# Transposing k, q and the attention result by DMA instead of on TensorE, in a fused attention and feed-forward kernel

## The chip, the cores and the metric

The kernel runs on one core of one Trainium2 chip. The metric is the device time of one execution, in microseconds (us). Every time is the median of some runs of the same program; every run here lists the core's mean granted TensorE clock and a state, and verdicts use fast runs alone. A ratio is the mean time of one kernel's fast runs over the mean of the other's fast runs in the same rounds, so it is not quite the ratio of the medians quoted.

Engine names in the profile: PE is TensorE's matmuls, PEld its weight loads, DVE is VectorE, ACT is ScalarE, POOL is GpSimd, and SP (SPq for its instruction queue) is SyncE.

## The reference

Sliding-window attention with a distance bias (8 batches, 8 heads, 576 positions, head size 64), then a feed-forward layer with a squared ReLU on the 4608 tokens.

```python
scores = scale * np.matmul(q, k.transpose(0, 1, 3, 2))
bias = slopes[:, None, None] * (-np.abs(rel).astype(np.float32))[None, :, :]
mask = (rel >= 0) & (rel < window)                  # window = 128
scores = np.where(mask, scores + bias[None], -1000000000.0)
attn = softmax(scores); attn_out = np.matmul(attn, v)
x = np.ascontiguousarray(attn_out.transpose(0, 2, 1, 3)).reshape(B * S, H * D)
h = x @ w_in                                        # 512 -> 2048
r = np.maximum(h, 0.0)
return ((r * r) @ w_out).astype(np.float32)         # 2048 -> 512
```
(softmax is written out in the original.) The kernel computes in bf16 with fp32 accumulation.

## The kernel before

Each batch has five blocks of positions (four of 128 and one of 64), 40 blocks in all. k and q of a block are loaded with positions on the partitions. Both must have the head dimension on the partitions, so TensorE transposes them against an identity into PSUM (eight 128x128 transposes, tile `tp`), and VectorE and ScalarE copy them out. q goes into `qp`, a tile with zeros in it, so that one matmul serves two heads. The attention result `x` of a block is transposed the same way (four transposes, tile `xp`) into `xT`, which the feed-forward layer reads.

```python
slot = Slot("h" if first else "att")
for i in range(2 * C):                               # C = 4
    def emit(i=i):
        ...
        nc.tensor.transpose(slot.tile[:, i * 128:(i + 1) * 128],
                            src[:, (i % C) * 128:(i % C + 1) * 128], ident)
    last = plan.add({"PE": mm(128)}, due - 56, emit, ...)
def evac_k():
    copy(t_k, kT[sk.idx][:, :, 0:n], slot.tile[:, 0:512]...)
t_k = plan.add(both if first else {"DVE": both["DVE"]}, due - 56, evac_k, [last], [], [slot])
for c2 in range(2):                                  # one half of qp on DVE, one on ACT
    def evac_q(c2=c2): ...
# ... scores, exp, mask, P x V, normalise into xt ...
for c in range(C):
    nc.tensor.transpose(slot_x.tile[:, c * 128:(c + 1) * 128], xt[sx.idx][:, c * 128:(c + 1) * 128], ident)
copy(t_xT[b, kb], xT[:, :, t0:t0 + n], slot_x.tile[:, 0:512]...)
```

Nothing is issued in the order of this text. Every operation is a task with an assumed duration, a key (its urgency) and the buffers that it takes and frees. A list scheduler in the kernel (class `Plan`) runs through assumed time and fixes, before the kernel starts, the order of instructions on every engine. An engine then works in that order and waits wherever the chip is later than the plan assumed.

The softmax here doesn't subtract the row's maximum and nothing guards it: scores larger than these inputs give would overflow.

Of the kernel before, what the change touches and what calls it, by code (L numbers as in the profile page):

```python
# [9 lines left out]
BF16 = mybir.dt.bfloat16  # L10
# [19 lines left out]
class Slot:  # L30


    def __init__(self, tag):
        self.tag, self.tile, self.left, self.freed, self.idx = tag, None, 0, 0.0, 0


class Plan:
# [18 lines left out]
    def order(self):  # L56
        used = {tag: [] for tag in self.bufs}
        free = {}
        cand = {}
        left = {}  # L60
        for t in self.tasks:
            left[t] = len(t.deps)
            for d in t.deps:
                d.users.append(t)
            for e in t.engs:
                free.setdefault(e, self.BEGIN.get(e, 800.0))
                cand.setdefault(e, [])
        for t in self.tasks:
            if not left[t]:
                for e in t.engs:  # L70
                    cand[e].append(t)

        def avail(t):
            at = t.ready
            for s in t.acq:
                u = used[s.tag]
                n = self.bufs[s.tag]
                if len(u) >= n:
                    old = u[len(u) - n]
                    if old.left:  # L80
                        return None
                    at = max(at, old.freed)
            return at

        done = []
        n_all = len(self.tasks)
        while len(done) < n_all:
            best = None
            for e, c in cand.items():
                lo = None  # L90
                for t in c:
                    a = avail(t)
                    if a is None:
                        continue
                    st = max(a, free[e])
                    k = (st, t.key, t.seq)
                    if lo is None or k < lo[0]:
                        lo = (k, t)
                if lo is not None and (best is None or lo[0][0] < best[0]):
                    best = (lo[0][0], e, lo[1])  # L100
            if best is None:
                raise RuntimeError("plan is stuck: " + repr([
                    (e, t.key, [s.tag for s in t.acq if avail(t) is None]) for e, c in cand.items() for t in c
                    if e != "POOL"][:40]))
            st, e, t = best
            t.eng, t.start = e, st
            dur = t.engs[e]
            if t.dma is not None:
                at = max(st + dur + 900.0, self.dma_free)
                self.dma_free = at + t.dma  # L110
                t.end = self.dma_free + 900.0
            else:
                t.end = st + dur + (self.LAT[e] if t.lat is None else t.lat)
            free[e] = st + dur
            for x in t.engs:
                cand[x].remove(t)
            for s in t.acq:
                s.idx = len(used[s.tag]) % self.bufs[s.tag]
                used[s.tag].append(s)
            for s in t.rel:  # L120
                s.left -= 1
                s.freed = max(s.freed, t.end)
            for u in t.users:
                left[u] -= 1
                u.ready = max(u.ready, st + dur if e == "PE" and "PE" in u.engs else t.end)
                if not left[u]:
                    for x in u.engs:
                        cand[x].append(u)
            done.append(t)
        done.sort(key=lambda t: (t.start, t.seq))  # L130
        return done
# [3 lines left out]
def kernel(  # L135
    ctx: ExitStack, tc: tile.TileContext, q, k, v, moe_w_in, moe_w_out, out
):
    nc = tc.nc

    B, H, S, D = q.shape  # L140
# [8 lines left out]
    C = d_model // 128  # L149
# [5 lines left out]
    psum = ctx.enter_context(tc.tile_pool(name="psum", bufs=2, space=bass.MemoryType.PSUM))  # L155
    work = ctx.enter_context(tc.tile_pool(name="work", bufs=2))

    ident = const.tile([128, 128], BF16)
# [5 lines left out]
    xT = const.tile([128, C, NT], BF16)  # L164

    def ring(name, n, shape):
        return [const.tile(shape, BF16, name=f"{name}_{i}") for i in range(n)]



    size = {"kn": 4, "qn": 4, "v": 6, "kT": 4, "qp": 3, "P": 3, "x": 2}
    kn = ring("kn", size["kn"], [128, d_model])
    qn = ring("qn", size["qn"], [128, d_model])
    vt = ring("vt", size["v"], [128, H, D + 1])
    kT = ring("kT", size["kT"], [128, C, 128])
    qp = ring("qp", size["qp"], [128, C, 2, 128])
    Pt = ring("P", size["P"], [128, H, 2, 128])
    xt = ring("x", size["x"], [128, d_model])

    plan = Plan({"h": 2, "o": 2, "s": 2, "att": 2, "rec": 4, "rt": 3, "g": 2, "osb": 3, **size})  # L180

    def act(n):
        return n * 0.84 + 55.0

    def dve(n, rate=1):
        return n / rate / 0.96 + 72.0

    def mm(n):
        return max(n, 64) / 2.4 + 1.5
# [12 lines left out]
    t_ident = plan.add({"DVE": 230.0}, -9e5 - 1, build_ident, [t_iota])  # L202
# [21 lines left out]
    t_zero = plan.add({"DVE": 2000.0}, -9e5, zero)  # L224
# [32 lines left out]
    s_in, t_in = {}, {}  # L257
# [23 lines left out]
    t_xT = {}  # L281
    chain = {"tp": [], "s": [], "pv": [], "xp": []}

    def copy(task, o, i):
        if task.eng == "DVE":
            nc.vector.tensor_copy(o, i)  # L286
        else:
            nc.scalar.activation(o, i, AF.Copy)  # L288

    def attention(m):  # L290
        b, kb = divmod(m, NKB)
        n = blk[kb]
        due = (b * S + kb * 128 + n) / 4 - 192 - 150
        first = b == 0


        sk, sq = Slot("kT"), Slot("qp")
        sk_of[m] = sk
        slot = Slot("h" if first else "att")
        last = None  # L300
        for i in range(2 * C):
            def emit(i=i):
                nm = "kq"[i // C]
                src = (kn if i < C else qn)[s_in[m, nm].idx]
                if i == 0:
                    slot.tile = psum.tile([128, 1024], BF16, tag=slot.tag, name="tp")
                nc.tensor.transpose(slot.tile[:, i * 128:(i + 1) * 128], src[:, (i % C) * 128:(i % C + 1) * 128],  # L307
                                    ident)
            last = plan.add({"PE": mm(128)}, due - 56, emit,
                            [last, t_ident, t_in[m, "kq"[i // C]]] + ([t_in[m, "q"]] + chain["tp"] if i == 0 else []),  # L310
                            [slot, sk, sq] if i == 0 else [], [s_in[m, "kq"[i // C]]] if i % C == C - 1 else [])
        chain["tp"] = [last]

        def evac_k():
            copy(t_k, kT[sk.idx][:, :, 0:n], slot.tile[:, 0:512].rearrange("p (c s) -> p c s", c=C)[:, :, 0:n])
        both = {"ACT": act(C * n), "DVE": dve(C * n, 2)}
        t_k = plan.add(both if first else {"DVE": both["DVE"]}, due - 56, evac_k, [last], [], [slot])
        t_q = []
        for c2 in range(2):
            def evac_q(c2=c2):  # L320
                po = c2 * 64
                o = qp[sq.idx][po:po + 64, :, c2, 0:n]
                i_ = slot.tile[po:po + 64, 512:1024].rearrange("p (c s) -> p c s", c=C)[:, :, 0:n]
                copy(t_q[c2], o, i_)
            t_q.append(plan.add(both if first else {"ACT": both["ACT"]} if c2 else {"DVE": both["DVE"]},
                                due - 56, evac_q, [last, t_zero], [], [slot]))
        t_k_of[m] = t_k


# [41 lines left out]
        sx = Slot("x")  # L371
        t_norm = []
        for hf in range(2):
# [32 lines left out]
            def norm(slot_v=slot_v, srec=srec, hf=hf):  # L406
# [5 lines left out]
                    op=ALU.mult)  # L412
            t_norm.append(plan.add({"DVE": dve(256)}, due - 12 + 4 * hf, norm, [t1] + t_norm,
                                   [], [slot_v, srec]))
        slot_x = Slot("o" if first else "att")
        last = None
        for c in range(C):
            def emit(c=c):
                if c == 0:
                    slot_x.tile = psum.tile([128, 1024], BF16, tag=slot_x.tag, name="xp")  # L420
                nc.tensor.transpose(slot_x.tile[:, c * 128:(c + 1) * 128],  # L421
                                    xt[sx.idx][:, c * 128:(c + 1) * 128], ident)
            last = plan.add({"PE": mm(128)}, due, emit, [last] + t_norm,
                            [slot_x] if c == 0 else [], [sx] if c == C - 1 else [])

        def evac():
            t0 = b * S + kb * 128
            copy(t_xT[b, kb], xT[:, :, t0:t0 + n],
                 slot_x.tile[:, 0:512].rearrange("p (c t) -> p c t", c=C)[:, :, 0:n])
        t_xT[b, kb] = plan.add(both if first else {"DVE": both["DVE"]}, due, evac, [last], [], [slot_x])  # L430

    sk_of, t_k_of = {}, {}
    for m in range(NBLK):
# [118 lines left out]
```

## Time and profile before

350.79 us, median of the 3 runs taken first (350.79 to 350.97).

| | before |
|---|---|
| PE busy, share of the span | 94% |
| DVE / ACT / POOL busy | 57% / 58% / 31% |
| share of PE in the chain of waits | 87% |
| tp and xp transposes in that chain | 4.8% and 2.3% |

The page of the kernel before: busy time by engine, the DMA queues (packets, megabytes, and the time their packets took as a share of 16 engines' span), and the chain of work that ended last.

```profile
...
PE 329.7 (94%) x2451; PEld 186.9 (54%) x2496; DVE 198.2 (57%) x600; ACT 203.2 (58%) x392; POOL 107.3 (31%) x133
...
q0 software_dynamic: 116736, 18.36, 72.0%
q1 hardware_dynamic: 5184, 9.44, 7.3%
...
PE 87%; DVE 6%; ACT 5%; issue 1%; ACTq 0%
PE o L483 34%; PE h L454 33%; PE ps_s L341 8%; PE tp L307 5%; PE pv L382 4%; PE xp L421 2%; ACT qp_90 L288 1%; DVE P_92 L367 1%; ACT masks L216 1%; ACT qp_91 L288 1%; ACT rt L462 1%; DVE x_96 L408 0%; ACT P_93 L359 0%; DVE qp_91 L286 0%; AC
...
```

TensorE bounds the kernel: it is busy 94% of the time and makes up 87% of the chain. The chain also prices the transposes: `tp` 5%, `xp` 2%.

The table by stage of the kernel before: for each stretch of time, its length, the busy time of each engine with the number of instructions, the granted clock, the DMA share (packet times summed over the 16 engines, so that overlapping packets can bring it above 1) and the GB/s.

```profile
...
50.00:78.00 28.00, 26.99 (x260) 17.39 (x265) 21.83 (x73) 19.96 (x41) 16.95 (x20) 1.00 1.71 123
78.00:130.00 52.00, 51.29 (x444) 30.79 (x450) 36.88 (x118) 34.10 (x69) 20.78 (x25) 1.00 1.06 89
130.00:175.00 45.00, 44.63 (x345) 25.57 (x350) 28.26 (x83) 27.95 (x54) 14.30 (x17) 1.00 0.75 73
175.00:215.00 40.00, 39.69 (x307) 22.83 (x312) 25.12 (x74) 24.53 (x47) 12.55 (x15) 1.00 0.78 72
...
```

DVE and ACT have room everywhere.

The timeline of the kernel before near 162 us (start, duration, engine, line, operation):

```profile
...
161.92 0.39 PE L307 MATMUL tp<-ident,kn_74 128*128 128x128 bf16 x4
...
162.14 0.39 PE L307 MATMUL tp<-ident,qn_78 128*128 128x128 bf16 x4
...
162.36 0.38 PE L454 MATMUL h<-xT,w_in_sb 128*128 128x512 bf16 x1
...
```

The eight transposes of one block take the time from 161.92 to 162.36, 0.44 us or some 55 ns each, and the next matmul follows at once.

### The profile page before, as it was taken

How to read it: one execution, taken by the hardware profiler on the slowest of the kernel's cores; microseconds unless marked ns; L12 is line 12 of the kernel's file. 1: busy time of each engine (PE TensorE's matmuls, PEld its weight loads, DVE VectorE, ACT ScalarE, POOL GpSimd, SP SyncE). 2: the span in 40 equal slices, each digit the busy share in tenths (PEclk: the TensorE clock that was granted, in tenths of full speed). 3: DMA queues.
4: the chain of work that ended last, by engine and by line, in shares of the span. 5: the costliest groups of instructions: out<-in, count | busy, mean ns of one | idle time of the engine just before them, and what ended most of it. 6: DMA issues, size and time to landing. Idle time of an engine off the chain costs nothing.

```text
span 349.0 us, 6481 instructions
## 1 busy us (share of the span) xinstructions
PE 329.7 (94%) x2451; PEld 186.9 (54%) x2496; DVE 198.2 (57%) x600; ACT 203.2 (58%) x392; POOL 107.3 (31%) x133
## 2 busy tenths in 40 slices
PE   2689999999999999999999999999999999999995
PEld 1565565576655555555555555555555444444442
DVE  6676796688876666656666566756666222222200
ACT  4585884886865666656665666755665344444411
POOL 8956747565534235232334234110000000000000
PEclk9999999999999999999999999999999999999999
DMA  9999999999999579595796867760000100110021
GB/s 76 141 198 162 165 192 154 87 118 74 123 102 85 62 76 92 62 84 62 73 92 67 78 68 73 73 68 31 30 15 33 48 30 32 38 52 32 30 84 66
DMA packets 121951, 28.20 MB, mean 81 GB/s; under 512 B 113217, under 2 KB 117313, under 8 KB 121921
## 3 DMA queue, kind: packets, MB, share of 16 engines
q0 software_dynamic: 116736, 18.36, 72.0%
q1 hardware_dynamic: 5184, 9.44, 7.3%
q8 instruction: 19, 0.31, 0.4%
q14 instruction: 12, 0.09, 0.1%
HBM read 36.70 MB, written 9.44 MB: 132 GB/s over the span
## 4 chain that ended last, share of the span: by engine, by line
PE 87%; DVE 6%; ACT 5%; issue 1%; ACTq 0%
PE o L483 34%; PE h L454 33%; PE ps_s L341 8%; PE tp L307 5%; PE pv L382 4%; PE xp L421 2%; ACT qp_90 L288 1%; DVE P_92 L367 1%; ACT masks L216 1%; ACT qp_91 L288 1%; ACT rt L462 1%; DVE x_96 L408 0%; ACT P_93 L359 0%; DVE qp_91 L286 0%; ACT P_92 L359 0%
## 5 line engine op out<-in xcount | busy, mean ns | idle before, releaser
L454 PE MATMUL h<-xT,w_in_sb 128*128 128x512 bf16 x557 | 158.7, 379 | 1.0
L483 PE MATMUL o<-w_out_sb,g 128*128 128x512 bf16 x550 | 150.2, 379 | 1.3
L462 ACT ACTIVATE rt<-h 128x512 bf16<-128x512 f32 x144 | 85.5, 596 | 66.2 <-PE h L454 62.4
L468 DVE TENSOR_TENSOR g<-rt 128x512 bf16<-128x512 bf16 x144 | 60.4, 420 | 62.0 <-ACT rt L462 59.9
L483 PEld LDWEIGHTS <-g 128*128 128x128 bf16 x576 | 54.1, 98 | 51.2
L454 PEld LDWEIGHTS <-w_in_sb 128*128 128x128 bf16 x576 | 54.3, 98 | 44.3 <-issue 0.2
L359 ACT ACTIVATE P_92<-ps_s 128x512 bf16<-128x512 f32 (+1 forms) x56 | 27.3, 506 | 12.2 <-PE ps_s L341 11.9
L494 ACT ACTIVATE osb<-o 128x512 f32<-128x512 f32 x36 | 21.5, 597 | 19.1 <-PE o L483 18.8
L359 ACT ACTIVATE P_94<-ps_s 128x512 bf16<-128x512 f32 (+1 forms) x52 | 26.0, 517 | 10.2 <-PE ps_s L341 9.8
L359 ACT ACTIVATE P_93<-ps_s 128x512 bf16<-128x512 f32 (+1 forms) x52 | 26.0, 517 | 9.7 <-PE ps_s L341 9.2
L367 DVE TENSOR_TENSOR P_92<-P_92,masks 128x512 bf16<-128x512 bf16 (+1 forms) x56 | 20.0, 363 | 8.6 <-ACT P_92 L359 8.2
L403 DVE RECIPROCAL rec<-pv 128x4 f32<-128x4 f32 (+1 forms) x80 | 14.0, 176 | 16.3 <-PE pv L382 15.8
L367 DVE TENSOR_TENSOR P_93<-P_93,masks 128x512 bf16<-128x512 bf16 (+1 forms) x52 | 19.0, 369 | 7.1 <-ACT P_93 L359 6.5
L367 DVE TENSOR_TENSOR P_94<-P_94,masks 128x512 bf16<-128x512 bf16 (+1 forms) x52 | 18.9, 368 | 6.2 <-ACT P_94 L359 5.8
L286 DVE COPY xT<-xp 128x512 bf16<-128x512 bf16 (+1 forms) x39 | 15.3, 393 | 8.5 <-PE xp L421 8.4
L408 DVE TENSOR_TENSOR x_95<-pv,rec 128x256 bf16<-128x256 f32 (+1 forms) x40 | 16.8, 419 | 0.7
L408 DVE TENSOR_TENSOR x_96<-pv,rec 128x256 bf16<-128x256 f32 (+1 forms) x40 | 16.6, 418 | 0.6
L268 POOL DMA_DIRECT2D kn_74<-in_k_dram x10 | 8.5, 845 | 19.7 <-PE tp L307 11.5
L382 PEld LDWEIGHTS <-P_92 128*128 128x128 bf16 x200 | 10.2, 99 | 6.0 <-DVE qp_90 L286 0.7
L268 POOL DMA_DIRECT2D kn_71<-in_k_dram x10 | 8.6, 863 | 14.2 <-PE tp L307 12.1
L268 POOL DMA_DIRECT2D kn_73<-in_k_dram x10 | 8.6, 862 | 13.2 <-PE tp L307 12.1
L382 PEld LDWEIGHTS <-P_93 128*128 128x128 bf16 x192 | 9.8, 101 | 4.7 <-DVE P_93 L367 0.3
(101 smaller groups left out, 403.5 us busy)
## 6 DMA issues: line engine op xcount, KB each, us to landing
out_dram<-osb SPq DMA_DIRECT2D x36, 256.0 KB, 2.0
w_in_sb<-in_moe_w_in_dram POOLq DMA_DIRECT2D x4, 512.0 KB, 10.2
w_out_sb<-in_moe_w_out_dram POOLq DMA_DIRECT2D x4, 512.0 KB, 9.9
kn_71<-in_k_dram POOLq DMA_DIRECT2D x8, 128.0 KB, 3.4
qn_75<-in_q_dram POOLq DMA_DIRECT2D x8, 128.0 KB, 4.4
kn_72<-in_k_dram POOLq DMA_DIRECT2D x8, 128.0 KB, 4.3
qn_76<-in_q_dram POOLq DMA_DIRECT2D x8, 128.0 KB, 4.2
kn_73<-in_k_dram POOLq DMA_DIRECT2D x8, 128.0 KB, 4.3
```

What stands on the lines that cost most here:

```text
L268: nc.gpsimd.dma_start(o, src[b, :, kb * 128:kb * 128 + n, :].rearrange("h s d -> s h d"))
L307: nc.tensor.transpose(slot.tile[:, i * 128:(i + 1) * 128], src[:, (i % C) * 128:(i % C + 1) * 128], ident)
L341: nc.tensor.matmul(slot_s.tile.rearrange("p (c t q) -> p c t q", c=2, t=2)[:, :, part, 0:n], kT[sk_of[mk].idx][:, c, :], qp[sq.idx][:, c, ...
L359: nc.scalar.activation(view(Pt[sP.idx][:, 2 * c:2 * c + 2]), view(slot_s.tile.rearrange("p (c t q) -> p c t q", c=2, t=2)), AF.Exp, bias=0 ...
L367: nc.vector.tensor_tensor(pt, pt, view(masks[:, 2 * c:2 * c + 2]), op=ALU.mult)
L382: nc.tensor.matmul(slot_v.tile[:, hi * (D + 1):(hi + 1) * (D + 1)], Pt[sP.idx][:, h, part, :], vt[s_in[mk, "v"].idx][:, h, :], start=part ...
L408: nc.vector.tensor_tensor(xt[sx.idx][0:n, hf * 256:(hf + 1) * 256].rearrange("p (h e) -> p h e", h=4), pv[0:n, :, 0:D], srec.tile[0:n, :]. ...
L454: nc.tensor.matmul(slot.tile, w_in_sb[:, cc, fc * 128:(fc + 1) * 128], xT[:, cc, g * 512:(g + 1) * 512], start=cc == 0, stop=cc == C - 1)
L462: nc.scalar.activation(srt.tile, slot.tile, AF.Relu, bias=0.0, scale=1.0)
L468: nc.vector.tensor_tensor(sg.tile[:, fc, :], srt.tile, srt.tile, op=ALU.mult)
L483: nc.tensor.matmul(slot.tile, sg.tile[:, fc, t * 128:(t + 1) * 128], w_out_sb[:, fc, :], start=fc == 0, stop=fc == FCB - 1)
L494: nc.scalar.activation(so.tile, slot.tile, AF.Copy)
```

## The change

The intent is to take the transposes off the engine that bounds the kernel. From the third batch on (30 of 40 blocks) k, q and the attention result are transposed by DMA from SBUF to SBUF, issued by SyncE, which before issued only the 36 output stores. The transposed q goes to a tile of its own, `qT`, and two VectorE copies spread it into the padded tile. The first two batches stay as they were. Cut to its core (the rest lets a buffer be taken by two tasks, and keeps the old code in an else branch):

```diff
-    size = {"kn": 4, "qn": 4, "v": 6, "kT": 4, "qp": 3, "P": 3, "x": 2}
+    size = {"kn": 4, "qn": 4, "v": 6, "kT": 4, "qT": 3, "qp": 3, "P": 3, "x": 3}
+        by_dma = b > 1
...
+        if by_dma:
+            def turn_k():
+                nc.sync.dma_start_transpose(kT[sk.idx], kn[s_in[m, "k"].idx])
+            t_k = plan.add({"SP": 100.0}, due - 80, turn_k, [t_in[m, "k"]], [sk], [s_in[m, "k"]], dma=500.0)
+            def turn_q():
+                nc.sync.dma_start_transpose(qT[st.idx], qn[s_in[m, "q"].idx])
+            t_t = plan.add({"SP": 100.0}, due - 80, turn_q, [t_in[m, "q"]], [st], [s_in[m, "q"]], dma=500.0)
+            for c2 in range(2):
+                def spread_q(c2=c2):
+                    po = c2 * 64
+                    nc.vector.tensor_copy(qp[sq.idx][po:po + 64, :, c2, 0:n], qT[st.idx][po:po + 64, :, 0:n])
...
+        if by_dma:
+            def turn_x():
+                nc.sync.dma_start_transpose(xT[:, :, t0:t0 + n], xt[sx.idx][0:n, :])
+            t_xT[b, kb] = plan.add({"SP": 100.0}, due, turn_x, t_norm, [], [sx], dma=500.0)
```

More of the change, by code (lines that the diff above doesn't have):

```diff
@@ L33, in __init__ @@
     def __init__(self, tag):
-        self.tag, self.tile, self.left, self.freed, self.idx = tag, None, 0, 0.0, 0
+        self.tag, self.tile, self.left, self.freed, self.idx = tag, None, 0, 0.0, None
 class Plan:
@@ L75, in avail @@
             for s in t.acq:
+                if s.idx is not None:
+                    continue
                 u = used[s.tag]
@@ L117, in order @@
             for s in t.acq:
+                if s.idx is not None:
+                    continue
                 s.idx = len(used[s.tag]) % self.bufs[s.tag]
@@ L175 @@
     kT = ring("kT", size["kT"], [128, C, 128])
+    qT = ring("qT", size["qT"], [128, C, 128])
     qp = ring("qp", size["qp"], [128, C, 2, 128])
@@ L294, in attention @@
         first = b == 0
+        by_dma = b > 1
         sk, sq = Slot("kT"), Slot("qp")
         sk_of[m] = sk
-        slot = Slot("h" if first else "att")
-        last = None
-        for i in range(2 * C):
-            def emit(i=i):
-                nm = "kq"[i // C]
-                src = (kn if i < C else qn)[s_in[m, nm].idx]
-                if i == 0:
-                    slot.tile = psum.tile([128, 1024], BF16, tag=slot.tag, name="tp")
-                nc.tensor.transpose(slot.tile[:, i * 128:(i + 1) * 128], src[:, (i % C) * 128:(i % C + 1) * 128],
-                                    ident)
-            last = plan.add({"PE": mm(128)}, due - 56, emit,
-                            [last, t_ident, t_in[m, "kq"[i // C]]] + ([t_in[m, "q"]] + chain["tp"] if i == 0 else []),
-                            [slot, sk, sq] if i == 0 else [], [s_in[m, "kq"[i // C]]] if i % C == C - 1 else [])
@@ L312, in attention, with emit, evac_k, evac_q @@
-        chain["tp"] = [last]
-        def evac_k():
-            copy(t_k, kT[sk.idx][:, :, 0:n], slot.tile[:, 0:512].rearrange("p (c s) -> p c s", c=C)[:, :, 0:n])
         both = {"ACT": act(C * n), "DVE": dve(C * n, 2)}
-        t_k = plan.add(both if first else {"DVE": both["DVE"]}, due - 56, evac_k, [last], [], [slot])
         t_q = []
-        for c2 in range(2):
-            def evac_q(c2=c2):
-                po = c2 * 64
-                o = qp[sq.idx][po:po + 64, :, c2, 0:n]
-                i_ = slot.tile[po:po + 64, 512:1024].rearrange("p (c s) -> p c s", c=C)[:, :, 0:n]
-                copy(t_q[c2], o, i_)
-            t_q.append(plan.add(both if first else {"ACT": both["ACT"]} if c2 else {"DVE": both["DVE"]},
-                                due - 56, evac_q, [last, t_zero], [], [slot]))
+        if by_dma:
+            st = Slot("qT")
+            def turn_k():
[8 more added lines that the diff above has]
+                    nc.vector.tensor_copy(qp[sq.idx][po:po + 64, :, c2, 0:n], qT[st.idx][po:po + 64, :, 0:n])
+                t_q.append(plan.add({"DVE": dve(C * n, 4)}, due - 56, spread_q, [t_t, t_zero],
+                                    [sq], [st]))
+        else:
+            slot = Slot("h" if first else "att")
+            last = None
+            for i in range(2 * C):
+                def emit(i=i):
+                    nm = "kq"[i // C]
+                    src = (kn if i < C else qn)[s_in[m, nm].idx]
+                    if i == 0:
+                        slot.tile = psum.tile([128, 1024], BF16, tag=slot.tag, name="tp")
+                    nc.tensor.transpose(slot.tile[:, i * 128:(i + 1) * 128], src[:, (i % C) * 128:(i % C + 1) * 128],
+                                        ident)
+                last = plan.add({"PE": mm(128)}, due - 56, emit,
+                                [last, t_ident, t_in[m, "kq"[i // C]]] + ([t_in[m, "q"]] + chain["tp"] if i == 0 else []),
+                                [slot, sk, sq] if i == 0 else [], [s_in[m, "kq"[i // C]]] if i % C == C - 1 else [])
+            chain["tp"] = [last]
+            def evac_k():
+                copy(t_k, kT[sk.idx][:, :, 0:n], slot.tile[:, 0:512].rearrange("p (c s) -> p c s", c=C)[:, :, 0:n])
+            t_k = plan.add(both if first else {"DVE": both["DVE"]}, due - 56, evac_k, [last], [], [slot])
+            for c2 in range(2):
+                def evac_q(c2=c2):
+                    po = c2 * 64
+                    o = qp[sq.idx][po:po + 64, :, c2, 0:n]
+                    i_ = slot.tile[po:po + 64, 512:1024].rearrange("p (c s) -> p c s", c=C)[:, :, 0:n]
+                    copy(t_q[c2], o, i_)
+                t_q.append(plan.add(both if first else {"ACT": both["ACT"]} if c2 else {"DVE": both["DVE"]},
+                                    due - 56, evac_q, [last, t_zero], [], [slot]))
@@ L414, in attention, with emit, evac @@
                                    [], [slot_v, srec]))
-        slot_x = Slot("o" if first else "att")
-        last = None
-        for c in range(C):
-            def emit(c=c):
-                if c == 0:
-                    slot_x.tile = psum.tile([128, 1024], BF16, tag=slot_x.tag, name="xp")
-                nc.tensor.transpose(slot_x.tile[:, c * 128:(c + 1) * 128],
-                                    xt[sx.idx][:, c * 128:(c + 1) * 128], ident)
-            last = plan.add({"PE": mm(128)}, due, emit, [last] + t_norm,
-                            [slot_x] if c == 0 else [], [sx] if c == C - 1 else [])
-        def evac():
-            t0 = b * S + kb * 128
-            copy(t_xT[b, kb], xT[:, :, t0:t0 + n],
-                 slot_x.tile[:, 0:512].rearrange("p (c t) -> p c t", c=C)[:, :, 0:n])
-        t_xT[b, kb] = plan.add(both if first else {"DVE": both["DVE"]}, due, evac, [last], [], [slot_x])
+        t0 = b * S + kb * 128
+        if by_dma:
+            def turn_x():
+                nc.sync.dma_start_transpose(xT[:, :, t0:t0 + n], xt[sx.idx][0:n, :])
+            t_xT[b, kb] = plan.add({"SP": 100.0}, due, turn_x, t_norm, [], [sx], dma=500.0)
+        else:
+            slot_x = Slot("o" if first else "att")
+            last = None
+            for c in range(C):
+                def emit(c=c):
+                    if c == 0:
+                        slot_x.tile = psum.tile([128, 1024], BF16, tag=slot_x.tag, name="xp")
+                    nc.tensor.transpose(slot_x.tile[:, c * 128:(c + 1) * 128],
+                                        xt[sx.idx][:, c * 128:(c + 1) * 128], ident)
+                last = plan.add({"PE": mm(128)}, due, emit, [last] + t_norm,
+                                [slot_x] if c == 0 else [], [sx] if c == C - 1 else [])
+            def evac():
+                copy(t_xT[b, kb], xT[:, :, t0:t0 + n],
+                     slot_x.tile[:, 0:512].rearrange("p (c t) -> p c t", c=C)[:, :, 0:n])
+            t_xT[b, kb] = plan.add(both if first else {"DVE": both["DVE"]}, due, evac, [last], [], [slot_x])
     sk_of, t_k_of = {}, {}
```

## The prediction

> **What bounds the kernel now.** TensorE. The page gives PE 94% busy against DVE 57%, ACT 58%, POOL 31%. In the table by stage PE is busy 24.8 of every 25 us from 100 us to 325 us, and 24.0 to 24.4 between 50 and 100 us. The chain of waits is 87% PE: o 34%, h 33%, ps_s 8%, tp 5%, pv 4%, xp 2%. So PE work that goes shortens the kernel, as long as what replaces it arrives in time.
>
> **Removed.** Of 40 blocks, 30 (batches 2 to 7) lose eight k/q transposes (tp) and four result transposes (xp): 360 matmuls. In the chain tp takes 4.8% of 349 us for 320 matmuls and xp 2.3% for 160; the timeline near 162 us shows eight tp in 0.44 us, 54 ns each. 360 x 54 ns = 19.4 us, nearly all of it on the chain. Per block DVE loses the copies to kT (395 ns), qp (390 ns) and xT (393 ns), ACT one copy to qp (540 ns).
>
> **Added.** Two VectorE copies per block, bf16 SBUF to SBUF, 64x512. I estimate 0.2 to 0.3 us each, under the 0.39 us that the same copy from PSUM takes. DVE and ACT both end up lighter; neither is the limit. Also added are 90 DMA transposes of up to 128x512 on SyncE's queue, which carries only 36 stores now. Their cost is the open point: the trace has none. The Trainium skill ("VectorE: DVE Perf Modes", the three transpose paths) gives 1309 ns for one 128x128 by DMA; "DMA: Bandwidth & Descriptors" (latency and other measured facts) gives 261 GB/s, which would make 128 KB an estimated 0.5 us of the DMA engines. No run here shows either yet. I expect 2 to 4 us from issue to landing and about 0.5 to 1.0 us of throughput each.
>
> **Does it fit?** After about 130 us it does: blocks come every 8 us, loads wait for buffers, and k and q are turned far ahead of use. Between 60 and 130 us it is tight. There the loads alone run in bursts at up to 155 GB/s (0.85 us per 128 KB load when queued), the new order puts about 15 blocks into some 60 us, and each needs about 2.3 us of loads plus three transposes. At 0.5 us a transpose this is 3.8 us per block and fits in the planned 3.9; at 1.0 us it is 5.3 us and costs about 20 us of PE waits, which would eat the gain, because PE's order is fixed in advance.
>
> **Prediction.** Full gain 350.8 - 19.4 = 331.4 us; I add 4 us of waits for early transposes: **335 us**, 8 in 10 between 329 and 356. Chances: faster by over 2% 0.66, within 2% 0.18, slower by over 2% 0.16.
>
> **What would show it.** Right: tp and xp each fall to a quarter; PE busy falls by about 19 us; h and o keep 379 ns mean and 0.215 us pace; PE's waits for kT or qp lie only before 130 us and sum to under 8 us; transposes land in under 4 us; loads still land in 3 to 6 us between 60 and 130 us. Wrong: ps_s waits on a DMA or on the copies into qp for tens of us; SyncE's queue is always occupied; loads land in 8 us or more; or h waits for xT.
>
> **What would make it wrong.** Transposes that go one at a time on the queue at 1.5 us or more, or that block the DMA engines for the loads; a transpose held behind a store or another transpose that waits on the in-order SyncE queue; GpSimd's descriptor writing slowed by the fast SBUF-to-SBUF copies.

## The result, and the profile after

334.5 us, median of 4 runs (333.18 to 334.81), against 350.79 us of 4 runs before; the ratio is 0.953 (95% interval 0.950 to 0.956). The kernel is 4.7% faster.

The page of the changed kernel, the same lines:

```profile
...
PE 308.0 (92%) x2098; PEld 164.8 (49%) x2136; DVE 182.3 (55%) x570; ACT 186.2 (56%) x362; POOL 107.4 (32%) x133
...
q0 software_dynamic: 116736, 18.36, 89.0%
q1 hardware_dynamic: 52608, 20.85, 34.0%
...
PE 79%; DMA 9%; DVE 5%; ACT 4%; issue 1%; ACTq 0%
PE o L511 34%; PE h L482 33%; PE ps_s L364 7%; DMA kT_87<-kn_73 5%; DMA kT_85<-kn_71 4%; PE pv L405 4%; PE tp L332 1%; DVE P_95 L390 1%; ACT masks L221 1%; ACT qp_93 L293 1%; ACT P_97 L382 1%; PE xp L450 0%; ACT P_95 L382 0%; DVE g L496 0%;
...
```

PE busy time fell from 329.7 to 308.0 us, by 21.7 us, but the span fell only from 349.0 to 333.0, by 16.0 us. So PE stands idle longer: 349.0 - 329.7 = 19.3 us before, 333.0 - 308.0 = 25.0 us after. (A few matmul records are missing from both traces, 2451 of 2496 before and 2098 of 2136 after by the count of weight loads, so these sums are good to a microsecond or two.) DMA, which had no share worth listing, is now 9% of the chain. The table by stage shows where:

```profile
...
50.00:78.00 28.00, 27.84 (x194) 14.83 (x195) 16.02 (x53) 15.99 (x32) 12.65 (x15) 1.00 1.98 156
78.00:130.00 52.00, 45.76 (x388) 26.34 (x392) 38.61 (x132) 32.76 (x68) 25.16 (x30) 1.00 2.16 164
130.00:175.00 45.00, 44.69 (x307) 23.91 (x312) 28.61 (x87) 27.47 (x54) 20.08 (x24) 1.00 1.82 168
175.00:215.00 40.00, 39.69 (x272) 21.18 (x277) 25.21 (x79) 23.75 (x47) 10.86 (x13) 1.00 1.36 126
...
```

Only one stage differs. Between 78 and 130 us PE is busy 45.76 of 52 us, where before it was 51.29. In the other stages it is as full as before. The chain of waits of the changed kernel in that stage (start, duration, what):

```profile
...
85.92 7.51 DMA kT_85<-kn_71
...
97.99 7.17 DMA kT_87<-kn_73
...
107.44 7.25 DMA kT_85<-kn_71
...
117.46 7.96 DMA kT_87<-kn_73
...
125.46 0.50 PE ps_s L364 x3
...
```

Four transposes of k, each 7.2 to 8.0 us from issue to landing, account for 29.9 of the 40 us from 85.9 to 125.5. The waits of PE's weight loads (what waited, for what, us in total, times, longest):

```profile
...
PEld L364 <- DMA kT_88<-kn_74: 3.0, 2, 2.0
PEld L364 <- DVE qp_92 L320: 2.0, 1, 2.0
PEld L364 <- DMA kT_87<-kn_73: 1.6, 2, 1.1
PEld L364 <- DMA kT_85<-kn_71: 1.3, 2, 1.0
PEld L364 <- DVE qp_93 L320: 0.7, 2, 0.5
PEld L364 <- DVE qp_94 L320: 0.2, 1, 0.2
...
```

They wait for kT, or for the copies into qp that wait for qT: 8.8 us in all, none longer than 2.0 us. (The matmuls behind them list such waits with 5.8 us in this window.) The timeline of SyncE in that stage:

```profile
...
99.61 1.30 SPq L315 DMA_TRANSPOSE qT_89<-qn_78  x1
101.00 1.27 SPq L441 DMA_TRANSPOSE xT<-x_98  x1
102.38 1.74 SPq L311 DMA_TRANSPOSE kT_88<-kn_74  x1
104.20 1.81 SPq L315 DMA_TRANSPOSE qT_90<-qn_75  x1
106.10 1.23 SPq L441 DMA_TRANSPOSE xT<-x_99  x1
107.44 1.72 SPq L311 DMA_TRANSPOSE kT_85<-kn_71  x1
...
```

SyncE issues one transpose after another and each issue occupies it for 1.2 us or more; the longest in this stage took 2.49 us, and those of k 1.64 us on average. From 78 to 130 us it was occupied by 38 DMAs (34 transposes and 4 stores) for 48.0 of 52 us. A store takes it 0.33 us at the median of the run, 0.53 us in this stage.

Two transposes of k by line, with the time that SyncE took to issue them (min/median/max, ns), and the time from issue to landing of all 30:

```profile
...
L311 SPq DMA_TRANSPOSE kT_87<-kn_73 x8: 1191/1264/1862, 51.9 to 214.9; - x8
...
L311 SPq DMA_TRANSPOSE kT_86<-kn_72 x7: 1207/1282/1622, 68.8 to 213.2; - x7
...
DMA to landing us min/median/max: 2.4/5.8/8.4
```

The best case, 2.4 us, is what a transpose takes on quiet DMA engines, the 1.2 us of its issue included (the transposes of x after 235 us all land in 2.3 to 2.4 us). Within 78 to 130 us the median is 7.0 us for k, 6.5 for q, 6.3 for x.

So the main account is short: 21.7 us of TensorE work gone, 5.7 us of new idle time, nearly all of it (5.5 us) in one crowded stage.

### The profile page after: what moved, and what is told of

Same layout as the page of the kernel before. It is cut to its first block, busy times and chain, and to the rows that moved or that the text cites. A ratio compares the mean times of both kernels' runs of the same rounds, so it can differ in the third digit from the quotient of the medians.

```text
span 333.0 us, 5942 instructions
## 1 busy us (share of the span) xinstructions
PE 308.0 (92%) x2098; PEld 164.8 (49%) x2136; DVE 182.3 (55%) x570; ACT 186.2 (56%) x362; POOL 107.4 (32%) x133
## 4 chain that ended last, share of the span: by engine, by line
PE 79%; DMA 9%; DVE 5%; ACT 4%; issue 1%; ACTq 0%
PE o L511 34%; PE h L482 33%; PE ps_s L364 7%; DMA kT_87<-kn_73 5%; DMA kT_85<-kn_71 4%; PE pv L405 4%; PE tp L332 1%; DVE P_95 L390 1%; ACT masks L221 1%; ACT qp_93 L293 1%; ACT P_97 L382 1%; PE xp L450 0%; ACT P_95 L382 0%; DVE g L496 0%; DVE x_100 L431 0%
## 5 line engine op out<-in xcount | busy, mean ns | idle before, releaser
L482 PE MATMUL h<-xT,w_in_sb 128*128 128x512 bf16 x554 | 152.6, 379 | 0.8
L522 ACT ACTIVATE osb<-o 128x512 f32<-128x512 f32 x36 | 21.5, 598 | 19.8 <-PE o L511 16.6
L426 DVE RECIPROCAL rec<-pv 128x4 f32<-128x4 f32 (+1 forms) x80 | 13.8, 176 | 16.7 <-PE pv L405 16.3
L273 POOL DMA_DIRECT2D kn_74<-in_k_dram x10 | 8.5, 845 | 25.2 <-DMA kT_88<-kn_74 8.7
L273 POOL DMA_DIRECT2D kn_73<-in_k_dram x10 | 8.5, 847 | 22.9 <-DMA kT_87<-kn_73 21.1
L405 PEld LDWEIGHTS <-P_95 128*128 128x128 bf16 x200 | 10.2, 99 | 5.1 <-DVE P_95 L390 0.3
L364 PEld LDWEIGHTS <-kT_88 128*128 128x128 bf16 x72 | 6.9, 98 | 11.0 <-DMA kT_88<-kn_74 3.0
L364 PEld LDWEIGHTS <-kT_86 128*128 128x128 bf16 x72 | 7.1, 99 | 10.4 <-issue 2.6
L431 DVE TENSOR_TENSOR x_98<-pv,rec 128x256 bf16<-128x256 f32 (+1 forms) x28 | 11.7, 418 | 0.4
L273 POOL DMA_DIRECT2D qn_77<-in_q_dram x10 | 8.5, 847 | 10.1 <-DMA qT_89<-qn_77 3.8
L364 PEld LDWEIGHTS <-kT_85 128*128 128x128 bf16 x72 | 7.2, 101 | 8.7 <-issue 1.6
```

Source lines behind the costliest of these rows:

```text
L273: nc.gpsimd.dma_start(o, src[b, :, kb * 128:kb * 128 + n, :].rearrange("h s d -> s h d"))
L364: nc.tensor.matmul(slot_s.tile.rearrange("p (c t q) -> p c t q", c=2, t=2)[:, :, part, 0:n], kT[sk_of[mk].idx][:, c, :], qp[sq.idx][:, c, ...
L405: nc.tensor.matmul(slot_v.tile[:, hi * (D + 1):(hi + 1) * (D + 1)], Pt[sP.idx][:, h, part, :], vt[s_in[mk, "v"].idx][:, h, :], start=part ...
L426: nc.vector.reciprocal(srec.tile[0:n, :], pv[0:n, :, D])
L431: nc.vector.tensor_tensor(xt[sx.idx][0:n, hf * 256:(hf + 1) * 256].rearrange("p (h e) -> p h e", h=4), pv[0:n, :, 0:D], srec.tile[0:n, :]. ...
L482: nc.tensor.matmul(slot.tile, w_in_sb[:, cc, fc * 128:(fc + 1) * 128], xT[:, cc, g * 512:(g + 1) * 512], start=cc == 0, stop=cc == C - 1)
```

## The experiments

The theory (P): the gain is TensorE time, less waits for late transposes in the crowded stage. The rival (V): the gain is relief of VectorE and ScalarE, which lose evacuations. Then, for the remaining loss: (A) the transposes share the DMA engines with the loads; (B) SyncE's in-order queue is full; (C) the plan crowds the blocks. All results were correct except where said. "Fast mean" below is the mean of the fast runs; that of the changed kernel is 334.2 us. The kernel before ran beside every group, at 349.97 to 350.8 us; so fast means of different groups compare to about 1 us, and the ratios are the safer measure.

| run | median us | fast mean us | ratio to before (95%) |
|---|---|---|---|
| changed kernel | 334.5 | 334.2 | 0.953 (0.950 to 0.956) |
| e1_x_only | 344.17 | 344.0 | 0.982 (0.981 to 0.984) |
| e2_kq_only | 337.52 | 337.5 | 0.964 (0.961 to 0.967) |
| e3_pe_back | 353.88 | 353.9 | 1.010 (1.009 to 1.012) |
| e4_dve_act_back | 342.55 | 339.9 | 0.971 (0.968 to 0.973) |
| f1_dve_act_clean | 335.88 | 336.6 | 0.961 (0.957 to 0.966) |
| e5_from_fifth | 336.82 | 336.8 | 0.962 (0.960 to 0.964) |
| e7_v_light (wrong on purpose) | 329.96 | 330.1 | 0.941 (0.939 to 0.944) |
| e9_sp_more | 345.26 | 344.7 | 0.983 (0.979 to 0.986) |
| e8_merged | 339.65 | 339.5 | 0.968 (0.964 to 0.972) |
| e6_plan_sp | 332.81 | 332.8 | 0.949 (0.946 to 0.952) |
| f5_paced | 333.32 | 333.2 | 0.951 (0.949 to 0.954) |
| f6_paced_sp_more | 341.83 | 341.1 | 0.976 (0.974 to 0.978) |

### e1_x_only and e2_kq_only: one part alone

```diff
 # e1_x_only, at the branch of k and q (they stay on TensorE)
-        if by_dma:
+        if False:
 # e2_kq_only: the same edit, at the branch of x (x stays on TensorE)
```

> Only the attention result is transposed by DMA; k and q stay on TensorE. Theory P (the gain is the TensorE time of the removed transposes, less what TensorE waits for late DMA transposes): 120 transposes x 54 ns = 6.5 us go, SyncE issues only one transpose per block so nothing waits: 344 to 345 us. Rival V (the gain comes from relieving VectorE and ScalarE and the PSUM buffers they hold): one of the three VectorE evacuations of 0.39 us goes, no ScalarE work; no firm number, but at least a third of the 16 us, so 345 or less, would have to come with VectorE; the two are told apart better by e3 and e4.

> Only k and q are transposed by DMA; the attention result stays on TensorE. Theory P: 240 transposes x 54 ns = 13.0 us go, and with two instead of three transposes per block on SyncE the waits of TensorE between 78 and 130 us shrink from about 5 us to under 2 us: 338 to 340 us. If the waits did not depend on how many transposes SyncE issues, they stay at 5 us: 343 us.

Measured: 344.2 and 337.5 us. Against 350.0 us of the kernel before on the same chip these are gains of 5.8 and 12.5 us, close to the 6.5 and 13.0 us of the removed TensorE time; e2 came out slightly better than expected. Together they gain 18.3 us, the whole change 16.3 us: the last third of the transposes on SyncE's queue costs some 2 us. In e2 no wait of PE for a kT is left. The trace of e2 shows 29 issues on SyncE from 78 to 130 us, 35.9 of 52 us, and PE busy 50.18 us there.

### e3_pe_back: only TensorE's work put back

```diff
+            # by_dma blocks: the same eight (and four) transposes into a PSUM tile that nobody reads
+            nc.tensor.transpose(slot_d.tile[:, i * 128:(i + 1) * 128], src[...], ident)
...
+            nc.tensor.transpose(slot_e.tile[:, c * 128:(c + 1) * 128], xt[sx.idx][...], ident)
```

> The changed kernel, with the twelve TensorE transposes per block added back into PSUM tiles that nobody reads; the DMA transposes still supply the data, VectorE and ScalarE stay relieved. Theory P: the 19 us come back, and the waits of the crowded stage are partly hidden under the added work: 348 to 354 us. Rival V: stays within 3 us of 334.5.

Measured: 353.9 us, slower than the kernel before, although VectorE and ScalarE keep their relief. The page of this run, busy time by engine:

```profile
...
PE 331.8 (94%) x2496; PEld 186.1 (53%) x2496; DVE 185.0 (52%) x570; ACT 187.1 (53%) x362; POOL 107.5 (31%) x133
...
```

PE is back to 331.8 us (before: 329.7), DVE and ACT stay at 185.0 and 187.1 us (before: 198.2 and 203.2). Rival V falls as the main cause; the gain follows TensorE. The added transposes also hold the input buffers longer, the fault that e4 below turns out to have; but PE's idle time is 352.5 - 331.8 = 20.7 us here, no more than in the changed kernel (25.0), so what came back is PE's work and not waiting.

### e4_dve_act_back and f1_dve_act_clean: only VectorE's and ScalarE's work put back

```diff
+            # per by_dma block, e4 reads qn and holds its buffer until all have run; f1 reads a constant tile
+            nc.vector.tensor_tensor(waste[:, i], a, a, op=ALU.mult)   # twice, 128x256
+            nc.scalar.activation(waste_a, a2, AF.Copy)                # once, 128x512
```

> The changed kernel, with two VectorE multiplies (128x256, about 0.29 us each) and one ScalarE copy (128x512, about 0.6 us) per block added back on scratch tiles, about what the change took from these two engines. Theory P: 334 to 336 us. Rival V: most of the 16 us comes back, 345 us or more.

> The test of e4 once more, without its fault: the two VectorE multiplies and the ScalarE copy per block read a constant tile, so they hold no q buffer and hold back no load. Theory P (TensorE time): 334 to 337 us. Rival V (relief of VectorE and ScalarE): 345 us or more. If it comes out near e4's 342.5, the work itself and not the held buffer did the damage.

e4 measured 342.6 us at the median, two of its four runs slow; its fast runs are 339.5 and 340.3 us. Neither theory had this. The scratch work read the q buffer and so freed it later. The one trace kept is of a slow run (344.8 us), so its chain of waits is a hint and no more (share of the span by line):

```profile
...
by line: PE o L523 30.7%; PE h L494 30.0%; PE ps_s L376 6.1%; DMA qn<-in_q_dram 4.6%; DMA qT<-qn 4.2%; DMA kT<-kn 3.4%; PE pv L417 3.1%; DVE P L402 2.3%; issue 1.8%; DVE x L443 1.3%; PE tp L344 1.2%; ACT qp L296 1.1%; DVE qp L332 0.8%; ACT
...
```

Loads of qn are 4.6% of that chain; in the changed kernel no load stands among its larger entries. e4 is a faulty test, since it delays loads as well. f1 reads a constant tile instead and measured 335.9 us (fast mean 336.6, one of four runs at 339.0), 2.4 us over the changed kernel (2.8 us by the ratios, whose intervals do not overlap), with DVE busy 190.2 and ACT 200.2 us. So rival V is out as the main cause; 2 to 3 of the 16 us may still belong to it, or to the somewhat different order of TensorE's work that the plan made for f1, which was not separated. By the fast runs e4 lies another 3.3 us above f1 (339.9 against 336.6): holding an input buffer longer, with the order that came of it, cost about as much as the work itself.

### e5_from_fifth: 20 blocks instead of 30

```diff
-        by_dma = b > 1
+        by_dma = b > 3
-  turn_k, [t_in[m, "k"]], [sk], ...          (turn_q likewise)
+  turn_k, [t_in[m, "k"]] + chain["tp"], [sk], ...
```
The added dependency only keeps the scheduler from a dead end.

> DMA transposes only from the fifth batch on (20 blocks), so not in the first part of the crowded stage. 240 transposes x 54 ns = 13.0 us go. Theory P with waits only from crowding: 337 to 339 us, TensorE waits for kT or qp under 1 us in all. If late transposes cost TensorE the same per block wherever they are, waits of some 3 us stay: 340 to 341 us.

Measured: 336.8 us, a gain of 13.2 us by the medians (350.0 before) for 13.0 us of removed TensorE time. The waits of PE list no DMA transpose and no copy from qT. Outside the first part of the crowded stage the transposes cost TensorE nothing that the trace shows; it is the crowd that costs.

### e7_v_light and e9_sp_more: loads against SyncE's queue

```diff
 # e7_v_light
-                nc.gpsimd.dma_start(o, src[b, :, ...])
+                e = 1 if nm == "v" and b > 1 else H          # one head of v instead of eight
+                nc.gpsimd.dma_start(o[:, 0:e], src[b, 0:e, ...])
 # e9_sp_more, once per by_dma block
+                nc.sync.dma_start_transpose(little[m % 4], ident[0:16, :])
```

> Wrong result on purpose: from the third batch on each load of v brings one head of eight, so about 30% of the load packets go; TensorE's and SyncE's orders are unchanged. Theory A (transposes land late, 7 us instead of 2.4 us, because they share the DMA engines with the loads): in the stage from 78 to 130 us transposes land in 3 to 5 us and TensorE's waits there fall by at least half: 330 to 332 us. Theory B (the in-order SyncE queue, 1.2 to 1.3 us per transpose whatever its size and back to back in that stage, is the limit): landing gets shorter but the waits stay within 1.5 us: 333.5 to 335 us.

> One small extra DMA transpose per block (16x128, 4 KB) whose result nobody uses; it costs SyncE's queue a whole issue but the DMA engines almost nothing; TensorE's order is unchanged. Theory B: SyncE then needs 4 issues x 1.3 us per block in the crowded stage, about 15 blocks, so up to 15 x 1.3 = 20 us more: 345 us or more, TensorE waits up by 10 us or more. Theory A: within 2 us of 334.5. If the small transpose is issued in much less than 1.2 us, the issue cost is not fixed and B predicts less.

e7 measured 330.0 us, as A said (330 to 332); B's forecast (333.5 to 335) fell. TensorE's weight loads come in the same order in e7, e9 and the changed kernel, so the runs compare directly. The table by stage of e7:

```profile
...
78.00:130.00 52.00, 50.02 (x424) 29.26 (x431) 41.90 (x142) 36.43 (x75) 25.77 (x35) 1.00 1.80 155
...
```

PE is busy 50.02 us there (changed kernel: 45.76). Transposes of k land in 4.4 us at the median in that stage, not 7.0, while SyncE is as occupied as before (40 issues, 47.8 of 52 us, against 48.0). Loads on the DMA engines lengthen the landings: q went from 6.5 to 4.5 us, x from 6.3 to 4.8. They lengthened issues too: those of k in this stage took 1.27 us on average, not 1.64. Why an issue gets longer beside loads was not tested.

e9 measured 345.3 us (three of four runs fast, mean 344.7), about what B said (345 or more) and far from A's forecast (within 2 us of 334.5). The small transposes, 4 KB each, by line:

```profile
...
L321 SPq DMA_TRANSPOSE little<-ident x30: 1162/1216/2887, 54.3 to 205.0; - x30
...
```

Their issue takes SyncE 1.2 us, just as one of 128 KB, and the 64-row transposes of x in the changed kernel take it 1.17 to 1.51 us, too. So an issue has a least price of about 1.2 us at either size, and 30 of them more cost 10.4 us (344.7 - 334.2) in a kernel whose TensorE order is the same. Landings did not get worse (k: 4.7 us at the median in the stage), so this is the queue and not the DMA engines. The table by time of e9 shows a second price:

```profile
...
80.00:90.00 10.00, 7.87 (x82) 1.00 2.11 107
90.00:100.00 10.00, 8.47 (x54) 0.66 1.61 172
100.00:110.00 10.00, 8.59 (x72) 1.00 1.96 170
...
```

From 90 to 100 us the granted clock was 0.66: PE stood idle from 87.9 to 91.3 us, and its clock was 0.50 from about 90.1 to 97 us. The Trainium skill ("TensorE: Matmul & The Clock Gate", Part 1) states that after an idle window of about 3.4 us TensorE goes to half its clock until it has been busy again for as long. In e9 the gap has that size, but the clock fell 2.2 us into it, and other traces do not agree. In e8 (below) the longest gap of PE in the stage was 2.1 us, from 112.3 to 114.4 us, and the clock was 0.50 from about 115.3 to 118.6 us:

```profile
...
110.00:120.00 10.00, 7.87 (x57) 0.83 1.76 170
...
```

In e5 it was 0.50 from 24 to 26.5 us, after no gap over 1.4 us, while in e6 a gap of 2.2 us (from 110.6 us) left it at 1.00. So idle time well under 3.4 us can cost clock, and these runs give no threshold. In the changed kernel no gap passes 1.6 us, and the clock stays at 1.00 in every stage. The rest of e9's surcharge over its waits was not taken apart.

Both A and B have a part: each transpose queues at SyncE first and at the DMA engines second, and the blocks follow each other through a few buffers, so delay in either place reaches TensorE. A full SyncE queue alone does not explain the loss, though: in e7 it was just as full, and PE's idle time in the stage fell from 6.2 to 2.0 us.

### e8_merged: k and q by one DMA

```diff
+    kqn = ring("kqn", size["kn"], [128, 2 * d_model]); kn, qn = its two halves
+    kqT = ring("kqT", size["kT"], [128, 2 * C, 128]);  kT = its first half, q is spread from the second
+                nc.sync.dma_start_transpose(kqT[sk.idx], kqn[s_in[m, "k"].idx])   # waits for both loads
```

> k and q of a block lie in one tile and are transposed by one DMA of 128x1024: the same bytes, two instead of three issues per block on SyncE. If the issue cost is fixed at 1.2 us, Theory B: SyncE is no longer full in the crowded stage, TensorE's waits there fall by at least half: 329 to 332 us. Theory A: no change, 333 to 336 us. If issuing 128x1024 takes 2.4 us, the cost goes with the size and both expect about 334 us. The order of TensorE's work differs somewhat.

Measured: 339.7 us, 5 us slower than the changed kernel, which nobody expected; B's forecast of 329 to 332 us fell. The issue of 256 KB took SyncE 1.41 us at the median (1.23 at least, 4.26 at most), so the least price hardly grows with the size; but the eleven issues of this kind in the crowded stage took 2.1 us on average. Two more things came with the merge: a transpose now waits for two loads, and the q half stays in its buffer until the last score that uses the k half. In the trace, which is of the fastest of the four runs (337.7 us), SyncE was occupied 43.0 us of the stage by 27 issues, 1.6 us each. PE was busy 47.58 of 52 us there, more than in the changed kernel, but with fewer matmuls (383 against 388) and a clock of 0.97; 2 us more were lost from 130 to 175 us (42.75 of 45). Which of these did it was not tested and stays open.

### e6_plan_sp: the plan told the price

```diff
-            t_k = plan.add({"SP": 100.0}, due - 80, turn_k, ...)      (turn_q, turn_x likewise)
+            t_k = plan.add({"SP": 1300.0}, due - 80, turn_k, ...)
```

> The kernel's own list scheduler is told that a DMA transpose holds SyncE for 1.3 us instead of 0.1 us; nothing else changes, so only the order of instructions does. If TensorE's waits come from an order that was built for transposes cheaper than they are, it places the scores later and more feed-forward work before them: waits in the stage from 78 to 130 us fall from about 5 us to under 2.5 us, 331 to 333 us. If the order does not matter, 334 to 335 us.

Measured: 332.8 us, ratio 0.949 (0.946 to 0.952) against 0.953 (0.950 to 0.956) of the changed kernel: the intervals overlap, so a gain of some 1.5 us is likely and not shown. PE is busy 47.50 instead of 45.76 us in the stage, so less came back than expected.

### f5_paced and f6_paced_sp_more: the blocks spread out

```diff
 # scores of block m, first matmul
+                if by_dma:
+                    tm.ready = 70000.0 + 6000.0 * (m - 2 * NKB)
 # f6: the same, with the small transpose of e9
```

> The list scheduler may not place the first score matmul of block m before 70 us + 6 us x (m - 10); all work is the same, only the order differs, and transposes are issued up to the same ring depth ahead. Theory C (the remaining loss comes from the scheduler crowding fifteen blocks into 60 us, where SyncE's queue is full and transposes land in 7 us): TensorE's waits between 78 and 130 us fall under 1.5 us, landing falls to 3 to 5 us: 328 to 331 us. If the loss is in the transposes themselves wherever they stand, 333 to 335 us.

> f5_paced with the small extra transpose of e9 per block; TensorE's order is that of f5_paced. Theory C: the extra issue finds room on SyncE's queue, within 2 us of f5_paced, against the 10.8 us that it cost in the crowded order. If an extra issue costs time by itself, 8 us or more over f5_paced.

f5 measured 333.3 us, which was not hoped for (it is the figure given for a loss that lies in the transposes themselves). Half of theory C held all the same. The waits of PE in f5:

```profile
...
PE h L484 <- DMA xT<-x: 3.9, 3, 1.8
PE ps_s L364 <- DVE qp L291: 3.4, 4, 1.4
...
```

No wait for kT or qT is left (the second line is of the first two batches, as before the change), and transposes of k land in 3.8 us at the median in the stage. But a new wait took their place: the feed-forward matmuls of the next group wait for xT, 3.9 us. With the blocks spread out, the last transpose of x of a group has nothing to spare. f6 measured 341.8 us (five of six runs fast, mean 341.1), 7.9 us over f5: theory C's expectation that an extra issue would find room fell. The trace is of the fastest of the six runs (338.3 us), so it shows only part of this. Its chain of waits:

```profile
...
95.32 0.28 DVE qp L326
...
95.62 0.30 DVE qp L326
95.92 0.40 SPq L317
...
96.38 1.22 SPq L321
...
97.68 0.53 SPq L538
...
98.31 3.18 DMA xT<-x
...
101.53 2.29 PE h L490 x5
...
```

The chain begins with VectorE's copies of an earlier q, but by SyncE's timeline the transpose of q after them was being issued from 95.10 us, without a gap before it and for its usual 1.22 us, so it did not wait for them. Behind it in SyncE's order stand the small transpose (1.22 us) and a store (0.53 us); the transpose of x that TensorE needs comes last. By the timeline VectorE had written the two halves of that x at 90.59 and 91.43 us, 0.42 us each, so the input was complete at 91.85 us; its transpose was issued at 98.31 us, 6.5 us later, after two stores, two small transposes and those of a k and a q. The in-order queue delayed the urgent DMA by what stood ahead of it.

None of these versions beats the changed kernel by more than the noise; e6 is the best correct one.

## Why the prediction was right

Predicted 335 us (329 to 356), measured 334.5 us.

- **What bounds the kernel, and what goes.** Right. 19.4 us of transposes were predicted to go; PE busy time fell by 21.7 us (why by 2.3 us more is not shown; at 55 ns the sum would be 19.8 us). e1, e2 and e5 gained 5.8, 12.5 and 13.2 us for an expected 6.5, 13.0 and 13.0 us; e3 gave it all back. The pace of h and o did not change: 379 ns mean, before and after.
- **VectorE and ScalarE are not the limit.** Right in the main, by e3 and f1 (putting their work back cost 2 to 3 us at most). The copies that spread q took 317 to 345 ns for 64x512, a little over the estimated 0.2 to 0.3 us. The Trainium skill ("VectorE: DVE Perf Modes", Rules for kernel authors) gives a dense bf16 copy within SBUF four results per cycle; here the gain over the copy of the same size from PSUM (412 to 416 ns in the kernel before) was only 16 to 24%. (The 390 ns of the prediction are a mean that includes the blocks of half the size.)
- **Waits of 4 us for early transposes, only before 130 us.** Nearly right, though the 4 us were a guess and not a sum: 5.7 us of new idle time, in the predicted stage, and the listed waits for kT and qp sum to 5.8 us at the matmuls and 8.8 us at the weight loads that precede them.
- **"I expect 2 to 4 us from issue to landing."** Wrong in size. On quiet engines it is 2.4 us, but the median is 5.5 to 5.8 us over the run and 7.0 us for k in the crowded stage. Likewise "loads still land in 3 to 6 us" failed: single loads landed in up to 9.7 us there.
- **"About 0.5 to 1.0 us of throughput each", and "at 1.0 us it is 5.3 us and costs about 20 us".** The throughput was right for the DMA engines: on quiet engines (241.5 to 245 us) the packets of one 128 KB transpose took 18.4% of 3.5 us of the 16 engines, 0.64 us. But the sum left out SyncE, whose 1.2 us or more for each issue, three per block and now and then a store, filled 48.0 of 52 us. In the changed kernel x transposes are issued at 83.1 us (block 11) and 128.4 us (block 21), so a block took (128.4 - 83.1) / 10 = 4.5 us against the planned 3.9. Ten blocks at 0.6 us more is 6 us, about the idle time that was found; that is an agreement of sizes and no proof. Issues run beside the loads, so the two do not simply add up: 2.3 + 3 x 1.2 = 5.9 us per block would have cost 20 us or more. They are not independent either, as e7 shows.
- **How much was luck.** Read with the 1.2 us that a transpose costs its queue, the prediction's own sum would have given up the whole gain; the plain expectation held because issues and loads overlap, which it had not considered. And two misses offset each other: PE's work fell by 2.3 us more than predicted, its idle time grew by 1.7 us more. The mechanism was right, but an error of half a microsecond is partly luck.
- **Signs of being wrong.** Two of the signs named did appear (a queue that is nearly always occupied in the stage, loads that land in 8 us or more) and the time was still right. They bear on one stage of 52 us; what they cost is to be read from PE's idle time there.
- **GpSimd's descriptor writing** was not slowed: issuing a load of k took 845 to 864 ns before and 845 to 861 ns after.

## What to carry to other kernels

Work taken off the engine that bounds a kernel is worth its time on that engine, as long as the replacement arrives; read the gain from the bounding engine's busy time and the loss from its new idle time, stage by stage. A DMA transpose of 128 KB took some 0.64 us of the DMA engines here but 1.2 us of the queue that issues it: count issues, and look at what stands ahead of the urgent one in that in-order queue. When an order is fixed in advance, try telling the scheduler the measured price of an issue (here some 1.5 us, within the noise), and look for a new wait where a crowd has been spread out, as in f5.

## What the Trainium skill lacked or had wrong

- "DMA: Bandwidth & Descriptors", Issuing engines are not separate DMA queues: it says that the sequencer time to initiate a DMA is usually small relative to the DMA. For a DMA transpose it is not: 1.2 us of SyncE against 2.4 us from issue to landing on quiet engines. A plain store takes SyncE 0.33 us.
- The same page names no trn2 price for issuing a transpose (its section on trn3 compares with "previous generations", without naming the chip). The runs show a least price that hardly depends on the size: 1.16 us for 4 KB, 1.19 us for 128 KB of k, 1.23 us for 256 KB. The medians are 1.22, 1.26 to 1.6 and 1.41 us, and single issues in the crowded stage took 2 us and more.
- "VectorE: DVE Perf Modes", the three transpose paths: 1309 ns for a 128x128 transpose by DMA can mislead if it is multiplied. Four times that data (128x512) lands in 2.4 us on quiet engines, and in 7.0 us (k, median) beside heavy loads; no page gives a figure for the second.
- "DMA: Bandwidth & Descriptors", Latency and other measured facts: 261 GB/s for transposes (of one kernel, with a non-contiguous middle dimension). No run here reaches a steady stream of transposes, so it is neither confirmed nor refuted; the queue's 1.2 us per 128 KB allows at most 109 GB/s (131072 bytes / 1.2 us) from one issuing queue at this size.
- "TensorE: Matmul & The Clock Gate", Part 1: the idle window of about 3.4 us is not what these runs show. The clock fell to 0.50 after a longest gap of 2.1 us in e8 and of 1.4 us in e5, and stayed at 1.00 after 2.2 us in e6.
